# Fused attention and two MoE layers: raw weights loaded from ScalarE's queue, v loaded from SyncE's, and product runs placed behind the scores

## The chip, the cores and the metric

The kernel runs on one NeuronCore of a Trainium2 chip, as one launch. The core has a matrix engine (TensorE, PE in the profile, whose weight loads are shown as PEld), VectorE (DVE), ScalarE (ACT), GpSimd (POOL) and SyncE (SP), which run side by side and wait for each other through semaphores. A DMA is issued by an engine's sequencer: SPq is SyncE's queue, ACTq ScalarE's. The metric is the time of one execution on the device in microseconds; a kernel's number is the median of its runs.

## The reference, cut to what matters

```python
scores = 1/sqrt(64) * q @ k.T                    # q, k, v: 4 batches, 8 heads, 576 rows, 64 columns
scores = where(scores >= max(scores) - tau, scores, -1e9)
attn = exp(scores - max(scores));  attn = attn / (sum(attn) + 1e-9)
x = heads_side_by_side(attn @ v)                 # 2304 tokens x 512
h = relu(x @ w_in);  x = (s * h*h + b) @ w_out   # the first two-layer stage, width 2048
h = x @ w2_in;  out = (h * tanh(softplus(h))) @ w2_out
```

The weights arrive as 64-bit floats. q, k, v are 32-bit.

## The kernel before, in words

**Attention.** Two heads are handled together as a pair; there are 16 pairs of 9 units. A unit's scores (`scores`, 4 or 8 matmuls of 288 columns, tile S) are read by VectorE (ns, with the row maximum), ScalarE takes exp (e), VectorE masks and sums, GpSimd scales. Seven units later `weights_t` transposes a block (T), ScalarE copies it out (te), and twice in a pair `products_v` multiplies: a run of 12 matmuls after block 6, a run of 8 after block 8, both into pv. `split_x` then rounds pv into a high part xh and a rest xl. Once in a pair, at units 2 and 4, `prep_qk` transposes the next pair's k and q (tpk, tpq), splits them (hik, lok, hiq, loq) and moves them into KH, KL and Q by DMAs of SyncE; the last of these DMAs is remembered as `self.moved`.

**First weights.** 32 pieces of w_in and w_out are converted by `split_w`, a generator that `split_all` advances by one step for each new piece. In step 0 a piece is loaded into a slot of tile wraw (four slots); in step 2 ScalarE scales its high words, in step 3 VectorE puts the words together in three operations (wa), in step 4 ScalarE rounds it (wp) and VectorE takes the rest. The first MoE stage of batch 0 multiplies straight from wp; a copy is stored in DRAM for the other batches. The first steps are taken during the attention of pairs 0 to 3, the others one for each 4 parts of the first MoE stage of batch 0.

**Order.** The first four pairs run alone (while the pool `s2p` is open). After that the attention of the later pairs and the first MoE stage (`moe1`, groups of 12 matmuls h and y) are traced side by side, in the proportion of their work, and the scheduler orders each engine's instructions by its own estimate of time. Each engine and each queue then runs its list in that order; one that waits holds all behind it. `issue_after(ins)` puts an instruction behind `ins` on the same engine; `keep_in_program_order` keeps the marked instructions of an engine in the order in which they are written. Two such rules matter here: in `split_w` the load of a piece stands behind `self.moved` on SyncE, and ScalarE's scaling is kept in program order. The second MoE stage (qX, qY, qV, o) follows from 782 us on.

**v.** `load_raw` loads a pair's v by three DMAs into one of two buffers. Pairs 0 and 1 are loaded at the start from SyncE; each later pair from ScalarE's queue, written behind the products of the pair that used the buffer last.

Of the kernel before, what the change touches and what calls it, by code (L numbers as in the profile page):

```python
# [19 lines left out]
class Fused:  # L20
# [26 lines left out]
    def split_w(self, src, hi, lo, pool, tags, kw):  # L47

        nc = self.nc
        i = self.nd
        self.nd += 1
        n = src.shape[1] * src.shape[2] // 2
        raw = pool.tile([P, n, 2], I32, tag=tags[0], name=f"wraw{i}", **kw)
        with self.tc.issue_after(self.moved):
            nc.sync.dma_start(raw.rearrange("p (c f) w -> p c (f w)", c=src.shape[1]), src)  # L60
        low, high = raw[:, :, 0], raw[:, :, 1]
        hf = high.bitcast(F32)
        yield
        yield
        a = pool.tile([P, n], I32, tag=tags[1], name=f"wa{i}")
        self.tc.keep_in_program_order(nc.scalar.activation(hf, hf, AF.Copy, scale=2.0 ** -112))
        yield
        nc.vector.tensor_scalar(a, high, 3, None, op0=ALU.logical_shift_left)
        nc.vector.scalar_tensor_tensor(a, low, 29, a, op0=ALU.logical_shift_right, op1=ALU.bitwise_or)
        nc.vector.scalar_tensor_tensor(a, high, -0x80000000, a, op0=ALU.bitwise_and, op1=ALU.bitwise_or)  # L70
        yield
        af = a.bitcast(F32).rearrange("p (c f) -> p c f", c=src.shape[1])
        nc.scalar.copy(hi, af)
        (nc.gpsimd if self.s2p else nc.vector).tensor_tensor(lo, af, hi.bitcast(F32), op=ALU.subtract)
# [159 lines left out]
    def load_raw(self, pr, nm):  # L234
        nc = self.nc
        b, p = divmod(pr, self.NP)
        if b >= self.B:
            return
        src = {"q": self.q, "k": self.k, "v": self.v}[nm]
        dma = nc.scalar if nm == "q" and not pr else nc.sync  # L240
        h2 = src[b, 2 * p:2 * p + 2]

        most = h2[:, 0:512, :].rearrange("h (p c) d -> p c h d", c=4)
        if nm == "v":
            t = self.vs[pr % 2]


            dma = nc.sync if pr < 2 else nc.scalar
            dma.dma_start(t[:, :, 0:4, :], most.rearrange("p c h d -> p h c d"))
            for h in range(2):  # L250
                dma.dma_start(t[HALVES[h], h, 4, :], h2[h, 512:576, :])
        else:
            t = self.qk[nm]
            dma.dma_start(t[:, 0:4], most)
            dma.dma_start(t[0:64, 4, :, :], h2[:, 512:576, :].rearrange("h r d -> r h d"))
        self.raws[pr, nm] = t
# [69 lines left out]
    def scores(self, pr, ti):  # L326
        nc = self.nc
        Q, KH, KL, E4 = self.sets[pr % 2]
        if ti == 0:
            self.st = self.at.tile([P, 5, 9], F32, tag="stat", name=f"st{pr}", bufs=2)  # L330
        st = self.st
        nm, nthr, sm, u, rinv = (st[:, i, :] for i in range(5))
        hs = [0] if ti < 4 else [1] if ti > 4 else [0, 1]
        cols = slice(512, 640) if ti == 4 else slice((ti % 5) * 128, (ti % 5) * 128 + 128)
        S = self.s_tile(f"S{pr}_{ti}")
        for hf in range(2):
            ks = slice(hf * 288, hf * 288 + 288)
            so = S[:, hf * HB:hf * HB + 288]
            terms = [(h, K[h]) for h in hs for K in (KH, KL)]
            for i, (h, kt) in enumerate(terms):  # L340
                c0 = ti * 128 + 64 * h if ti <= 4 else 64 + ti * 128
                nc.tensor.matmul(so, Q[:, c0:c0 + 128], kt[:, ks], start=(i == 0), stop=(i == len(terms) - 1))  # L342
        ns = self.at.tile([P, 576], F32, tag="ns", name=f"ns{pr}_{ti}", bufs=2)
        sv = S.rearrange("p (h n) -> p h n", h=2)[:, :, :288]
        c1 = slice(ti, ti + 1)
        nc.vector.tensor_scalar(ns.rearrange("p (h n) -> p h n", h=2), sv, -0.125, 3.0e38,  # L346
                                op0=ALU.mult, op1=ALU.min, accum_out=nm[:, c1])
        nc.vector.tensor_scalar(nthr[:, c1], nm[:, c1], self.tau_c, None, op0=ALU.add)

        if ti < 4:  # L350
            self.es[pr, ti, "pair"] = self.at.tile([P, 1152], F32, tag="e", name=f"e{pr}_{ti}", bufs=8)
        e = E4[:, 64:640] if ti == 4 else self.es[pr, ti % 5, "pair"][:, 0 if ti < 4 else 576:][:, :576]
        nc.scalar.activation(e, ns, AF.Exp, bias=nm[:, c1], scale=-1.0)  # L353
        self.es[pr, ti] = e

        def finish():
            nc.vector.scalar_tensor_tensor(e, ns, nthr[:, c1], e, op0=ALU.is_le, op1=ALU.mult, accum_out=sm[:, c1])  # L357
            if ti not in (1, 4, 8):
                return
            g = slice({1: 0, 4: 2, 8: 5}[ti], ti + 1)  # L360
            nc.vector.tensor_scalar(rinv[:, g], sm[:, g], 1.0e-9, None, op0=ALU.add)
            nc.vector.reciprocal(rinv[:, g], rinv[:, g])  # L362

            nc.vector.tensor_scalar(u[:, g], sm[:, g], 0.5, 1.0 / self.S, op0=ALU.is_lt, op1=ALU.mult)
            for j in range(g.start, g.stop):
                t = self.es[pr, j]
                nc.gpsimd.tensor_scalar(t, t, rinv[:, j:j + 1], u[:, j:j + 1], op0=ALU.mult, op1=ALU.add)  # L367

        return finish
# [24 lines left out]
    def products_v(self, pr, chunks, tes, first, last):  # L394

        if first:
            self.pv = self.pvp.tile([P, 1024], F32, tag="pv", name=f"pv{pr}")
        v = self.vs[pr % 2]
        ins = None
        for c in chunks:  # L400
            for hf, h in ((0, 1), (0, 0), (1, 1), (1, 0)):
                te = tes[4 if c == 4 else c + 5 * h]
                args = (self.pv[HALVES[h], hf * HB:hf * HB + 288], v[:, h, c, :], te[:, hf * 288:hf * 288 + 288])
                kw = dict(start=first and c == chunks[0], stop=last and c == chunks[-1])
                if ins is None:
                    ins = self.nc.tensor.matmul(*args, **kw).ins
                else:
                    with self.tc.issue_after(ins):
                        ins = self.nc.tensor.matmul(*args, **kw).ins  # L409
        return ins  # L410
# [11 lines left out]
    def attention(self):  # L422
# [3 lines left out]
        nc = self.nc  # L426
# [14 lines left out]
        for k in range(N + LAG + 2):  # L441
            pr, ti = divmod(k, 9)
            if k < N:
                nxt = self.scores(pr, ti)
                if k < 12:
                    self.busy(warm[:, :256], 3)
                if fin:
                    fin()
                fin = nxt
                yield 550  # L450
                if pr + 1 < self.B * self.NP and ti in (2, 4):
                    self.prep_qk(pr + 1, "kq"[ti // 2 - 1])
                    yield 500
            elif fin:
                fin()
                fin = None
            j = k - LAG
            run = None
            if todo:
                tp, tc, te = todo  # L460
                tes[tc] = te
                if tc == 6:
                    run = self.products_v(tp, (1, 4, 0), tes, True, False)
                    yield 1460
                elif tc == 8:
                    run = self.products_v(tp, (3, 2), tes, False, True)
                    yield 970
                    self.split_x(tp)
                    self.load_raw(tp + 2, "v")
            todo = None  # L470
            if 0 <= j < N:
                prj, ci = divmod(j, 9)
                todo = prj, ci, self.weights_t(prj, ci, run)
                yield 550
# [461 lines left out]
```

## Time and profile before

| | |
|---|---|
| time, median of 3 runs | 1146.13 us (1144.81 to 1146.3) |
| profiled execution, its own time | 1139.95 us |
| its span, first to last instruction | 1138.2 us |
| mean granted clock of TensorE | 0.993 |
| busy: PE, DVE, ACT, POOL | 1084.1, 791.6, 620.6, 256.4 us |

A span is divided in stages by what runs: 0 to 140 us attention alone, 140 to 320 attention beside batch 0 of the first MoE stage with the conversion of its weights, 320 to 660 attention beside batches 1 and 2, 660 to 682 the last attention, 682 to 782 batch 3, and from 782 the second MoE stage. In the views, a wait is the idle time of an engine before an instruction, and behind the arrow stands what ended it. Line numbers are those of the kernel before.

### The profile page before, as it was taken

How to read it: one execution, taken by the hardware profiler on the slowest of the kernel's cores; microseconds unless marked ns; L12 is line 12 of the kernel's file. 1: busy time of each engine (PE TensorE's matmuls, PEld its weight loads, DVE VectorE, ACT ScalarE, POOL GpSimd, SP SyncE). 2: the span in 40 equal slices, each digit the busy share in tenths (PEclk: the TensorE clock that was granted, in tenths of full speed). 3: DMA queues.
4: the chain of work that ended last, by engine and by line, in shares of the span. 5: the costliest groups of instructions: out<-in, count | busy, mean ns of one | idle time of the engine just before them, and what ended most of it. 6: DMA issues, size and time to landing. Idle time of an engine off the chain costs nothing.

```text
span 1138.2 us, 21403 instructions
## 1 busy us (share of the span) xinstructions
PE 1084.1 (95%) x7964; PEld 1018.2 (89%) x7964; DVE 791.6 (70%) x1746; ACT 620.6 (55%) x1153; POOL 256.4 (23%) x306
## 2 busy tenths in 40 slices
PE   7887999998899999999999989999999999999998
PEld 7765789887798989899889879999999999999998
DVE  5988766879776676867776767654787377825782
ACT  4656686756566656557646557643454144513351
POOL 3543334252332433415243210300000000000000
PEclk9999999999999999999999999999999999999999
DMA  7376385656887678887974589985999999997783
GB/s 160 87 180 187 103 239 186 227 158 215 237 275 250 213 222 247 286 256 241 328 228 138 193 299 341 394 340 217 351 387 346 335 413 387 338 338 260 265 296 121
DMA packets 141591, 292.70 MB, mean 257 GB/s; under 512 B 52848, under 2 KB 78960, under 8 KB 133168
## 3 DMA queue, kind: packets, MB, share of 16 engines
q1 hardware_dynamic: 134256, 286.91, 74.9%
q10 hardware_dynamic: 7232, 4.43, 1.4%
q8 instruction: 63, 1.03, 0.4%
q14 instruction: 40, 0.33, 0.1%
HBM read 201.85 MB, written 66.58 MB: 236 GB/s over the span
## 4 chain that ended last, share of the span: by engine, by line
PE 59%; DVE 8%; DMA 6%; ACT 3%; issue 2%; POOL 2%; SPq 1%; DVEq 0%; ACTq 0%; POOLq 0%
PE o L747 16%; PE y L502 11%; PE h L502 9%; PE qY L613 7%; PE qX L613 4%; PE qV L613 4%; PE pv L409 2%; PE S L342 2%; DMA wsi<-chli 2%; PE T L380 2%; POOL e L367 1%; DVE e L357 1%; DMA wso<-chlo 1%; DVE ns L346 1%; DMA wraw<-in_moe_w_out_dram 1%
## 5 line engine op out<-in xcount | busy, mean ns | idle before, releaser
L367 POOL TENSOR_SCALAR e<-e,st 128x576 f32<-128x576 f32 x128 | 134.1, 1059 | 212.1 <-DVE st L362 187.4
L747 PE MATMUL o<-wo,hl 128*128 128x256 f32 x1512 | 177.9, 279 | 0.0
L747 PEld LDWEIGHTS o<-wo,hl 128*128 128x128 f32 x1512 | 177.5, 188 | 0.0
L502 PE MATMUL h<-xh,w 128*128 128x288 f32 x768 | 164.5, 299 | 4.4 <-ACT r L523 1.4
L502 PE MATMUL y<-gh,w 128*128 128x288 f32 x768 | 165.5, 300 | 0.0
L357 DVE SCALAR_TENSOR_TENSOR e<-ns,st,e 128x576 f32<-128x576 f32 x128 | 118.6, 927 | 36.0 <-ACT e L353 35.2
L346 DVE TENSOR_SCALAR_CACHE_REDUCE ns<-S 128x576 f32<-128x576 f32 x144 | 107.8, 751 | 48.8 <-PE S L342 48.3
L353 ACT ACTIVATE e<-ns,st 128x576 f32<-128x576 f32 x128 | 99.0, 776 | 65.4 <-DVE ns L346 55.3
L502 PEld LDWEIGHTS h<-xh,w 128*128 128x128 f32 x768 | 125.7, 188 | 7.1 <-ACT r L523 2.6
L502 PEld LDWEIGHTS y<-gh,w 128*128 128x128 f32 x768 | 127.1, 190 | 0.1
L526 POOL TENSOR_TENSOR gl<-rr,gh 128x288 fp32r<-128x288 f32 x96 | 85.6, 898 | 171.3 <-ACT rr L525 165.8
L391 ACT COPY te<-T 128x576 f32<-128x576 f32 x144 | 91.4, 635 | 58.8 <-PE T L385 42.1
L502 PE MATMUL y<-gl,w 128*128 128x288 f32 x384 | 114.4, 298 | 1.8 <-POOL gl L526 1.8
L502 PE MATMUL h<-xl,w 128*128 128x288 f32 x384 | 113.5, 296 | 0.0
L380 PE MATMUL T<-ident,e 128*128 128x128 f32 x576 | 96.6, 284 | 16.0 <-ACT te L391 12.6
L342 PE MATMUL S<-KH,Q 128*128 128x288 f32 x320 | 96.9, 320 | 12.2 <-DVE ns L346 4.7
L380 PEld LDWEIGHTS T<-ident,e 128*128 128x128 f32 x576 | 69.4, 144 | 35.7 <-issue 16.3
L342 PE MATMUL S<-KL,Q 128*128 128x288 f32 x320 | 90.8, 300 | 0.0
L409 PE MATMUL pv<-te,rawv 128*64 128x288 f32 x576 | 87.2, 410 | 0.0
L613 PE MATMUL qY<-yc,wi 128*128 128x384 f32 x432 | 86.6, 337 | 0.7 <-DVE g L636 0.7
L342 PEld LDWEIGHTS S<-KH,Q 128*128 128x128 f32 x320 | 62.0, 194 | 19.3 <-DVE ns L346 7.6
L613 PEld LDWEIGHTS qY<-yc,wi 128*128 128x128 f32 x432 | 75.6, 188 | 1.3 <-DVE g L636 1.3
(150 smaller groups left out, 2186.8 us busy)
## 6 DMA issues: line engine op xcount, KB each, us to landing
w<-w SPq DMA_DIRECT2D x96, 512.0 KB, 5.5
wo<-wso SPq DMA_DIRECT2D x42, 1024.0 KB, 7.4
wi<-wsi SPq DMA_DIRECT2D x23, 1024.0 KB, 7.8
wi<-wsi SPq DMA_DIRECT2D x25, 768.0 KB, 7.3
w<-wp SPq DMA_DIRECT2D x32, 512.0 KB, 5.0
wsi<-chli SPq DMA_DIRECT2D x24, 512.0 KB, 5.0
wso<-chlo SPq DMA_DIRECT2D x24, 512.0 KB, 6.2
ycd<-yp SPq DMA_DIRECT2D x14, 768.0 KB, 7.8
```

Source lines behind the costliest of these rows:

```text
L342: nc.tensor.matmul(so, Q[:, c0:c0 + 128], kt[:, ks], start=(i == 0), stop=(i == len(terms) - 1))
L346: nc.vector.tensor_scalar(ns.rearrange("p (h n) -> p h n", h=2), sv, -0.125, 3.0e38, op0=ALU.mult, op1=ALU.min, accum_out=nm[:, c1])
L353: nc.scalar.activation(e, ns, AF.Exp, bias=nm[:, c1], scale=-1.0)
L357: nc.vector.scalar_tensor_tensor(e, ns, nthr[:, c1], e, op0=ALU.is_le, op1=ALU.mult, accum_out=sm[:, c1])
L367: nc.gpsimd.tensor_scalar(t, t, rinv[:, j:j + 1], u[:, j:j + 1], op0=ALU.mult, op1=ALU.add)
L380: nc.tensor.transpose(T[:, i * 128:i * 128 + 128], self.es[pr, i, "pair"][:, o:o + 128], self.ident)
L391: nc.scalar.copy(te, T[:, :576])
L409: ins = self.nc.tensor.matmul(*args, **kw).ins
L502: nc.tensor.matmul(acc[:, :n], w[:, wl, c], rhs[c][xl][:, ts], start=(i == 0), stop=(i == 11))
L526: (nc.vector if b == 3 else nc.gpsimd).tensor_tensor(gl[:, ts], r2, gh[:, ts].bitcast(F32), op=ALU.subtract)
L613: self.nc.tensor.matmul(acc, a, b, start=(first and i == 0), stop=(i == n - 1), skip_group_check=True)
L747: nc.tensor.matmul(bank[p][t], hl[:, gl, j, ts], w[:, 2 * (q % 2) + j, wl], start=(old is None and q + j + k == 0), stop=(q + j + k == 6), ...
```

## The change

Three things are changed. The load of a raw weight piece is issued by ScalarE and kept in its program order, where it was issued by SyncE behind the last k or q move. v is loaded by SyncE for every pair, for pairs 2 to 14 behind the k moves of the next pair (at unit 2 of the pair itself), for pair 15 at its unit 2, where it was loaded by ScalarE behind the products two pairs before. And the first matmul of a product run stands behind the last scores traced so far, once the first four pairs are over.

```diff
@@ split_w
-        with self.tc.issue_after(self.moved):
-            nc.sync.dma_start(raw.rearrange("p (c f) w -> p c (f w)", c=src.shape[1]), src)
+        self.tc.keep_in_program_order(nc.scalar.dma_start(raw.rearrange("p (c f) w -> p c (f w)", c=src.shape[1]), src))
@@ load_raw
-            dma = nc.sync if pr < 2 else nc.scalar
@@ scores
-                nc.tensor.matmul(so, Q[:, c0:c0 + 128], kt[:, ks], start=(i == 0), stop=(i == len(terms) - 1))
+                self.scored = nc.tensor.matmul(so, Q[:, c0:c0 + 128], kt[:, ks], start=(i == 0), stop=(i == len(terms) - 1)).ins
@@ products_v
-                    ins = self.nc.tensor.matmul(*args, **kw).ins
+                    with self.tc.issue_after(self.scored) if not self.s2p else nullcontext():
+                        ins = self.nc.tensor.matmul(*args, **kw).ins
@@ attention
+                if pr + 1 == self.B * self.NP and ti == 2:
+                    self.load_raw(pr, "v")
                 if pr + 1 < self.B * self.NP and ti in (2, 4):
                     self.prep_qk(pr + 1, "kq"[ti // 2 - 1])
+                    if ti == 2 and pr >= 2:
+                        with self.tc.issue_after(self.moved):
+                            self.load_raw(pr, "v")
...
                     self.split_x(tp)
-                    self.load_raw(tp + 2, "v")
```

The built lists of the engines show what moves. First SyncE's queue in the kernel before, at the k and q moves of pair 7 (wraw13 to wraw16 are weight pieces, rawq is a later pair's q, w1 a stored piece):

```order
L303 DMA KL11_130<-lok7_2176 64x576
L60 DMA wraw13_2202<-in_moe_w_in_dram 128x4x256
L60 DMA wraw14_2271<-in_moe_w_out_dram 128x4x256
L254 DMA rawq_111<-in_q_dram 128x8x64
L255 DMA rawq_111<-in_q_dram 64x2x64
L303 DMA Q1_125<-hiq7_2303 64x576 x2
L303 DMA Q1_125<-loq7_2304 64x576 x2
L60 DMA wraw15_2367<-in_moe_w_out_dram 128x4x256
L60 DMA wraw16_2425<-in_moe_w_out_dram 128x4x256
L195 DMA w1_0_2_1_2508<-wp0_2_1_2192 128x1024
```

Pieces 13 and 14 stand behind the k moves, 15 and 16 behind the q moves. In the changed kernel the same loads stand on ScalarE, each behind the scaling (L65) of the piece two before it; here two steps in a row:

```order
L72 CAST wp0_2_2_2579<-wa18_2771 128x512
L65 ACTIVATE wraw20_2773<-wraw20_2773 128x512
L59 DMA wraw22_2936<-in_moe_w_out_dram 128x4x256
L525 ACTIVATE gh0_2_1_2659<-r0_2_1_0_2696 128x288
L526 ACTIVATE rr0_2_1_0_2697<-r0_2_1_0_2696 128x288
L278 CAST hiq7_2303<-tpq7_2294 128x640
L525 ACTIVATE gh0_2_1_2659<-r0_2_1_1_2734 128x288
L526 ACTIVATE rr0_2_1_1_2735<-r0_2_1_1_2734 128x288
L72 CAST wp0_2_3_2670<-wa19_2854 128x512
L65 ACTIVATE wraw21_2856<-wraw21_2856 128x512
L59 DMA wraw23_3014<-in_moe_w_out_dram 128x4x256
```

The rounding (L72) of piece 18, whose slot piece 22 takes, is ahead of that load. At the q of pair 7 ScalarE is at piece 22, where SyncE's queue before was at piece 15. On SyncE the three v loads of a pair stand behind the k moves of the next pair, ahead of the next q load (here pair 8's last k move, pair 7's v, two stores of pieces, then a q load):

```order
L299 DMA KL01_122<-lok8_2785 64x576
L245 DMA rawv1_136<-in_v_dram 128x2x256
L247 DMA rawv1_136<-in_v_dram 64x64 x2
L194 DMA w1_1_2_3_3505<-wp1_2_3_3147 128x1024
L194 DMA w1_0_3_2_3587<-wp0_3_2_3231 128x1024
L250 DMA rawq_111<-in_q_dram 128x8x64
```

Before, these three loads stood on ScalarE's queue. On TensorE, the first product run of pair 5 before, which follows the transposes of pair 7's q; the scores S6_5 come 27 rows behind its first row:

```order
L274 MATMUL tpq7_2294<-ident_72,rawq_111 128x64
L272 MATMUL tpq7_2294<-ident_72,rawq_111 128x128 x4
L274 MATMUL tpq7_2294<-ident_72,rawq_111 128x64
L406 MATMUL pv5_2369<-te5_6_2324,rawv1_136 64x288
L409 MATMUL pv5_2369<-te5_1_2007,rawv1_136 64x288
```

And in the changed kernel, where the same run follows those scores:

```order
L503 MATMUL y0_1_1_0_2839<-gh0_1_3_2494,wp1_1_1_2357 128x288
L338 MATMUL S6_5_2334<-KH01_120,Q0_117 128x288
L338 MATMUL S6_5_2334<-KL01_122,Q0_117 128x288
L338 MATMUL S6_5_2334<-KH01_120,Q0_117 128x288
L338 MATMUL S6_5_2334<-KL01_122,Q0_117 128x288
L403 MATMUL pv5_2369<-te5_6_2324,rawv1_136 64x288
```

The scores of a unit are issued about one unit earlier against products and transposes, in every pair after the fourth.

## Rows read from the trace of the kernel before

**Rows 1.** The page: busy time by engine; then the last-ending chain by engine.
```profile
PE 1084.1 (95%) x7964; PEld 1018.2 (89%) x7964; DVE 791.6 (70%) x1746; ACT 620.6 (55%) x1153; POOL 256.4 (23%) x306
PE 59%; DVE 8%; DMA 6%; ACT 3%; issue 2%; POOL 2%; SPq 1%; DVEq 0%; ACTq 0%; POOLq 0%
```

**Rows 2.** Windows: stretch, length; busy PE, PEld, DVE, ACT, POOL; clock; DMA; GB/s.
```profile
0.00:140.00 140.00, 115.28 (x782) 95.08 (x783) 110.60 (x328) 79.52 (x122) 57.94 (x85) 0.95 0.56 142
140.00:320.00 180.00, 166.86 (x1266) 151.86 (x1265) 139.49 (x346) 120.38 (x238) 62.75 (x82) 1.00 0.69 211
320.00:660.00 340.00, 332.47 (x2522) 306.85 (x2521) 242.60 (x606) 212.09 (x426) 124.53 (x131) 0.99 0.75 238
660.00:682.00 22.00, 18.12 (x134) 14.48 (x134) 11.97 (x25) 10.88 (x19) 0.00 (x0) 1.00 0.96 344
782.00:1138.20 356.20, 351.99 (x2520) 350.85 (x2518) 225.78 (x330) 138.05 (x213) 0.00 (x0) 1.00 0.87 321
```

**Rows 3.** Waits of PE from 140 to 320: total us, times, longest us.
```profile
PE tpq L274 <- DVE ns L346: 3.3, 2, 2.4
PE T L380 <- ACT te L391: 2.9, 2, 2.3
PE S L342 <- DVE ns L346: 2.0, 2, 1.2
PE y L502 <- ACT wp L73: 1.5, 1, 1.5
PE y L502 <- ACT r L523: 1.4, 1, 1.4
```

**Rows 4.** Timeline of SyncE's queue: start, length, instruction.
```profile
255.89 1.75 SPq L60 DMA_DIRECT2D wraw<-in_moe_w_out_dram  x3
```

**Rows 5.** Chain that ended last, in order of time: start, length, what.
```profile
243.81 4.79 DMA wraw<-in_moe_w_in_dram
248.62 0.68 ACT wraw L66
249.32 0.43 DVE wa L68
```

**Rows 6.** Timeline of PE, three instructions that waited: idle time and releaser in brackets.
```profile
250.47 0.43 PE L274 MATMUL tpq<-ident,rawq 128*128 128x64 f32 x2 [2.42 <-DVE ns L346]
...
264.83 0.40 PE L502 MATMUL y<-gh,wp 128*128 128x288 f32 x1 [1.45 <-ACT wp L73]
...
312.19 0.66 PE L380 MATMUL T<-ident,e 128*128 128x128 f32 x4 [2.34 <-ACT te L391]
```

**Rows 7.** Waits of ACT and DVE for the raw weights, 140 to 320.
```profile
ACT wraw L66 <- DMA wraw<-in_moe_w_out_dram: 14.0, 10, 2.9
...
DVE wa L68 <- ACT wraw L66: 16.9, 8, 3.9
```

**Rows 8.** Tiles rawv and wraw: issues (ns min/median/max, first, last), landing time.
```profile
L251 ACTq DMA_DIRECT2D rawv<-in_v_dram x28: 472/514/1303, 47.1 to 592.5; - x28
L249 ACTq DMA_DIRECT2D rawv<-in_v_dram x14: 368/372/464, 53.8 to 602.4; - x14
...
L60 SPq DMA_DIRECT2D wraw<-in_moe_w_in_dram x16: 367/504/964, 61.7 to 268.2; - x16
...
DMA to landing us min/median/max: 3.8/5.6/9.4
```

**Rows 9.** Timeline of ACT: an exp that stood behind a v load.
```profile
128.57 0.77 ACT L353 ACTIVATE e<-ns,st 128x576 f32<-128x576 f32 x1 [4.56 <-PE pv L409]
```

**Rows 10.** Timeline of SyncE's queue, moves of pair 3's q and what precedes them.
```profile
61.73 0.59 SPq L60 DMA_DIRECT2D wraw<-in_moe_w_in_dram  x1
```

**Rows 11.** Waits of PE from 320 to 660.
```profile
PE y L502 <- POOL gl L526: 1.8, 1, 1.8
...
PE T L380 <- POOL e L367: 1.0, 2, 0.6
PE T L380 <- ACT te L391: 1.0, 2, 0.7
```

## The prediction

> **What bounds the kernel now.** I read the page's busy line and chain first, then the windows by stage, then TensorE's waits inside the one stage that the change touches most, and from there the queue that caused them. TensorE is busy 95% and has 59% of the chain [rows 1], so the time can fall only where TensorE idles. The windows say where that is [rows 2]: idle is length less PE busy, 24.7 us before 140 us, 13.1 from 140 to 320, 7.5 from 320 to 660, 3.9 from 660 to 682, and 4.2 in the 356 us after 782. The change cannot reach the last stage. No engine beside TensorE is full in the middle stages: VectorE is busy 139.5 of 180 us and ScalarE 120.4 [rows 2]. So the 13.1 us are waits for something late, not for something overloaded.
>
> What is late is the weight conversion. The reader is to follow one case. SyncE issues a raw piece at 243.81, right behind the k moves; it lands 4.79 us later, ScalarE scales it at 248.62 and VectorE starts on it at 249.32 [rows 5]. VectorE's list is in order, so the read of a score tile behind it waits too, and the tile is what TensorE needs: it stands still 2.42 us and starts at 250.47 [rows 6]. The next burst is three loads at 255.89 [rows 4]; it ends in 1.45 us without wp at 264.83 [rows 6]. The third ends in 2.34 us without a free transpose tile at 312.19, since ScalarE's copy stood behind a scaling whose piece had not landed [rows 6]. In the stage ScalarE waits 14.0 us in 10 waits for w_out pieces, VectorE 16.9 us in 8 for the scaling [rows 7]. Loads take a median of 5.6 us to land [rows 8]; they are late because they are issued late, two to six at a time behind a pair's moves.
>
> **Raw loads on ScalarE.** This removes the pin behind the moves and adds 32 issues to ScalarE's list. Each load now stands right behind the scaling of the piece two before it, so it has one whole step and part of another, and a step is 180 us over some 24 pieces, 7.5 us. Against a landing of 5.6 us [rows 8] that is enough, with some 5 us over on average. The slot is free by then: its rounding is ahead in the list. Bounds for the gain: 0, if VectorE's total work of 139.5 us re-forms the same waits elsewhere, and 13.1 us, all idle of the stage [rows 2]. The three cases followed add up to 6.2 us (2.42 + 1.45 + 2.34) [rows 6], and the waits for ns of 3.3 and 2.0 and for r of 1.4 [rows 3] hold others of the same kind, made by the bursts. I take 7.0 us, between the three cases and the whole, near the cases.
>
> The issues themselves: 32 of 0.504 us [rows 8] are 16.1 us of ScalarE's sequencer. The v loads that leave it were 28 of 0.514 and 14 of 0.372 us [rows 8], 19.6 us. ScalarE gets 3.5 us lighter over the kernel, but the weight-conversion stage gets heavier: 24 of the issues, 12.1 us, against some 5 pairs of v loads of 1.4 us, 7.0 us. These 5.1 us lie beside 59.6 us in which ScalarE is idle there [rows 2]. I cost them at nothing; without that cover they are 5.1 us.
>
> The Trainium skill, page "DMA: Bandwidth & Descriptors", section "Issuing engines are not separate DMA queues", says that DMAs issued from ScalarE, SyncE and GpSimd run on the same 16 engines and interleave, and that issuing from several saves no more than sequencer time. By that sentence the change gives nothing but issue time, which is off TensorE's path, and the sum would be zero for this part. The trace agrees that the transfers are not what is scarce (the DMA engines are busy 0.69 of the stage [rows 2]), but what it shows as late is the moment of issue, 243.81, behind other entries [rows 5], which the sentence does not price. The rival of no change below has its own price from rows.
>
> **v on SyncE.** It takes from ScalarE the waits in which it stood behind a v load until products had ended. The longest of the prologue is 4.56 us before an exp [rows 9]. Bounds for one such wait: 0, since the transposed block that ScalarE copies next stands behind the same products on TensorE anyway, and 4.56. Most are of the first kind; I take 1.0 us for all. On SyncE the loads are three issues, 1.4 us by the durations on ScalarE [rows 8], behind the k moves and ahead of the next q load. With pair 3 SyncE is issuing without a pause and the weight load in that place took 0.59 us [rows 10], so q's moves there come 0.8 us later, and these are waited for. Later pairs find SyncE idle ahead of the q load. The buffer of v is free then, the products that read it being over four units before, so nothing queues behind a wait, and v is used 12 units later. Together 0.2 us gained, rounded to 0.
>
> **Products behind scores.** No instruction is added. A run of 12 or 8 matmuls moves behind 4 or 8 score matmuls, so the scores, and with them the chain from ns to e to the transposes, get about one unit of lead. What can go are waits of transposes for e and te from 320 to 660: 1.0 for POOL's e and 1.0 for te [rows 11], 2.0 us. The bounds: 7.5 us gained, all the stage's idle [rows 2], and 2.0 lost, if the score tile, of which there is one, makes VectorE's read the new wait; the waits for ns that this would copy were 2.0 us in the weight stage [rows 3]. The 1.8 us for gl [rows 11] is a MoE wait and stays. I take 2.0 us gained. The tail from 660 to 682 idles 3.9 us [rows 2]; a group or two of MoE matmuls remains as filler beside the last transposes. I take 1.0, from 0 to 3.9.
>
> **Sum.** 7.0 + 0 + 2.0 + 1.0 = 10.0 us, from 1139.95 us of the profiled execution (span 1138.2 and 1.75 us around it) to 1129.95. That execution was 6.18 us shorter than the median of the runs, 1146.13. The time to be compared is such a median, so the same 10.0 us are taken from it: **1136.1 us**.
>
> **Rivals.**
> - More goes: the bursts also made the waits for ns and r, the prologue loses part of its 24.7 us, and the tail goes whole. All of 13.1, 7.5 and 3.9 is 24.5 us, 1121.6. For it: no engine is full. Against it: VectorE is busy 110.6 of the first 140 us [rows 2], and a schedule with three new orders makes new small waits. I price it at 20 us, 1126. Chance 0.12.
> - No change: VectorE does the same 139.5 us in the weight stage, and what it no longer waits for the loads it waits for elsewhere, or the change is issue time and no more. That is 1146.1. Against it stand the followed cases, in which both ScalarE and VectorE were idle. Chance 0.11.
> - Slower: ScalarE is held by its own loads. In the built lists 24 of the 32 carry a wait for the semaphore of an earlier DMA, most of them SyncE's k, q or v loads and moves, which in turn wait for TensorE. If the earlier DMA has not landed, te, exp, r and wp stand behind the load. A ScalarE wait of that kind cost TensorE 2.34 us at 312.19 [rows 6]. From 5 such holds on, the gain is gone (5 x 2.34 = 11.7); a third of the 24, 8 holds, is 18.7 us less 10.0, 8.7 slower: 1154.8. For it: v loads on the same queue did hold ScalarE by 4.56 us [rows 9]. Against: in the lists, the awaited DMA was mostly issued some ten ScalarE instructions earlier. Chance 0.13.
>
> **How the numbers follow.** The forecast has 0.64. Its own range, from half the sum to the sum with the stage's whole 13.1, is 1130 to 1141. The range that holds 8 in 10 reaches up over the case of no change, 1148, and down to where half of the rival of more lies, 1124. A difference under 0.2%, 2.3 us, can't be told from none here. Faster: 0.64 + 0.12 = 0.76; same 0.11; slower 0.13.
>
> **What the profile after would show.** Right: raw loads on ScalarE's queue one by one, each landed before its scaling, so that ScalarE's and VectorE's waits for raw pieces fall from 14.0 and 16.9 us [rows 7] to a few; TensorE's idle in the weight stage under 7 us; transposes of the later stages without waits for POOL's e; the stage from 782 as long as before, 356 us. Wrong: idle of TensorE put down to te, r or wp with ScalarE standing before a raw load's issue; or the raw waits gone while TensorE's idle stays near 13 us with VectorE full; or new waits of score matmuls for ns after 320 us, which would say that the earlier scores only moved the wait.

## The result, and the profile after

The changed kernel takes 1131.27 us (median of 4 runs, 1130.48 to 1133.57) against 1145.47 us for the kernel before in the same series (4 runs, 1138.06 to 1146.3): ratio 0.9894, 95% interval 0.9865 to 0.9924. That is 8.7 to 15.5 us faster; the forecast was 1136.1 us, 10.0 us faster. The kernel before scatters: in the later series, 17 runs each, it took 1136.6 to 1148.1 us, with medians from 1142.93 to 1143.75. Its profiled execution, 1139.95, lies in the lower part of that scatter. The profiled execution of the changed kernel, 1133.57 us with a span of 1131.8, is the longest of its runs. The two profiles are therefore 6.4 us apart, less than the medians.

The page of the changed kernel (busy time, then the chain of work that ended last) beside [rows 1]:

```profile
PE 1081.1 (96%) x7964; PEld 1018.7 (90%) x7964; DVE 806.3 (71%) x1746; ACT 619.0 (55%) x1153; POOL 263.4 (23%) x306
PE 67%; DVE 3%; DMA 3%; ACT 2%; issue 1%; POOL 0%; DVEq 0%; ACTq 0%; POOLq 0%
```

DMA's share of the chain went from 6% to 3%, VectorE's from 8% to 3%, and SyncE's queue, 1% before, is gone from it. The windows of the changed kernel, in the stretches of [rows 2], then the whole first part and the last stage by its own bounds (columns: stretch, length; busy PE, PEld, DVE, ACT, POOL; clock; DMA share; GB/s):

```profile
0.00:140.00 140.00, 110.64 (x738) 90.35 (x738) 107.14 (x314) 75.21 (x114) 52.84 (x79) 0.91 0.60 151
140.00:320.00 180.00, 176.97 (x1361) 163.93 (x1360) 158.47 (x368) 123.94 (x246) 74.42 (x88) 1.00 0.74 226
320.00:660.00 340.00, 332.35 (x2539) 307.49 (x2539) 251.20 (x614) 216.87 (x436) 127.11 (x131) 0.99 0.73 237
660.00:682.00 22.00, 18.05 (x136) 15.94 (x133) 11.97 (x24) 13.52 (x33) 0.00 (x0) 1.00 0.95 359
0.00:772.78 772.78, 728.17 (x5444) 667.64 (x5444) 580.46 (x1416) 480.29 (x940) 263.36 (x306) 0.98 0.73 231
772.78:1131.80 359.02, 352.91 (x2520) 351.09 (x2520) 225.80 (x330) 138.75 (x213) 0.00 (x0) 1.00 0.85 319
```

And the last two of the kernel before by its own bounds:

```profile
0.00:781.70 781.70, 731.82 (x5445) 667.01 (x5445) 565.83 (x1416) 482.30 (x940) 256.40 (x306) 0.99 0.72 228
781.70:1138.20 356.50, 352.29 (x2520) 351.15 (x2520) 225.78 (x330) 138.32 (x213) 0.00 (x0) 1.00 0.87 321
```

TensorE's idle time is length less busy. From 140 to 320 it fell from 13.1 to 3.0 us. Before 140 us it rose from 24.7 to 29.4. From 320 to 660 (7.5, now 7.7) and from 660 to 682 (3.9, now 4.0) it did not move. In the whole first part the idle time fell by 5.3 us (49.9 to 44.6) and TensorE's busy time by 3.7 (731.8 to 728.2), and the last stage became 2.5 us longer: 5.3 + 3.7 - 2.5 = 6.5, the difference of the spans (6.4) but for rounding. A window with fixed bounds holds other work in another kernel, as the counts in brackets show, so the sums over the whole first part weigh more than those of one stage.

What became of the weight pieces is read best from the tile wraw, where the view says who waited for it (us, times). The kernel before, whole span, then the changed kernel:

```profile
  DVE wa L68: 21.5, 9
  ACT wraw L66: 19.7, 14
  ACT wp L73: 8.6, 10
```

```profile
  ACT wp L72: 3.3, 2
  DVE wa L67: 2.4, 1
```

ScalarE's scaling (L66 before, L65 now) no longer waits for a piece at all. ScalarE's timeline in the changed kernel shows why (start, length, engine and line; idle before in brackets):

```profile
222.23 0.37 ACTq L59 DMA_DIRECT2D wraw<-in_moe_w_out_dram  x1
...
223.23 0.69 ACT L65 ACTIVATE wraw<-wraw 128x512 f32<-128x512 f32 x1
...
226.51 0.37 ACTq L59 DMA_DIRECT2D wraw<-in_moe_w_out_dram  x1
...
233.55 0.38 ACTq L59 DMA_DIRECT2D wraw<-in_moe_w_in_dram  x1
...
234.19 0.68 ACT L65 ACTIVATE wraw<-wraw 128x512 f32<-128x512 f32 x1
```

One load stands in each step, and the piece loaded at 222.23 is scaled two steps later, at 234.19, 12 us after its issue. The piece of [rows 5] was scaled 4.8 us after its issue, when it had just landed. Of TensorE's waits from 140 to 320, where [rows 3] had 3.3, 2.9, 2.0, 1.5 and 1.4 us, these are left:

```profile
PE S L338 <- DVE lok L279: 1.0, 1, 1.0
PE tpq L270 <- DVE ns L342: 0.9, 1, 0.9
PE y L503 <- DVE y L550: 0.5, 1, 0.5
PE y L503 <- ACT r L524: 0.4, 1, 0.4
PE pv L403 <- ACT te L387: 0.2, 1, 0.2
```

### The profile page after: what moved, and what is told of

It is laid out like the page before. It is cut to its first block, busy times and chain, and to the rows that moved or that the text cites. A ratio compares the mean times of both kernels' runs of the same rounds, so it can differ in the third digit from the quotient of the medians.

```text
span 1131.8 us, 21384 instructions
## 1 busy us (share of the span) xinstructions
PE 1081.1 (96%) x7964; PEld 1018.7 (90%) x7964; DVE 806.3 (71%) x1746; ACT 619.0 (55%) x1153; POOL 263.4 (23%) x306
## 4 chain that ended last, share of the span: by engine, by line
PE 67%; DVE 3%; DMA 3%; ACT 2%; issue 1%; POOL 0%; DVEq 0%; ACTq 0%; POOLq 0%
PE o L748 16%; PE y L503 13%; PE h L503 12%; PE qY L614 6%; PE qX L614 4%; PE qV L614 4%; PE S L338 3%; PE pv L406 3%; PE T L376 3%; DMA wso<-chlo 1%; DMA wi<-wsi 1%; PE pv L403 1%; PE T L381 1%; DMA w<-w 1%; ACT e L349 0%
## 5 line engine op out<-in xcount | busy, mean ns | idle before, releaser
L353 DVE SCALAR_TENSOR_TENSOR e<-ns,st,e 128x576 f32<-128x576 f32 x128 | 114.9, 899 | 22.6 <-ACT e L349 21.6
L527 POOL TENSOR_TENSOR gl<-rr,gh 128x288 fp32r<-128x288 f32 x96 | 93.6, 989 | 128.8 <-ACT rr L526 128.8
L376 PE MATMUL T<-ident,e 128*128 128x128 f32 x576 | 92.5, 283 | 15.3 <-ACT te L387 14.7
```

Source lines behind the costliest of these rows:

```text
L376: nc.tensor.transpose(T[:, i * 128:i * 128 + 128], self.es[pr, i, "pair"][:, o:o + 128], self.ident)
L527: (nc.vector if b == 3 else nc.gpsimd).tensor_tensor(gl[:, ts], r2, gh[:, ts].bitcast(F32), op=ALU.subtract)
```

## The experiments

All times are medians; a ratio is that of the runs to the runs of the kernel before in the same series, with its 95% interval. Three theories stood against each other. A: the gain is the weight pieces that no longer land late. B: it is the scores ahead of the product runs. C: it is ScalarE without v's loads.

**raw_only**, the first part of the change alone:

```diff
-        with self.tc.issue_after(self.moved):
-            nc.sync.dma_start(raw..., src)
+        self.tc.keep_in_program_order(nc.scalar.dma_start(raw..., src))
```

> Only the raw weight loads are moved to ScalarE; v's loads and the product runs are as before. Theory A (the gain is the weight pieces that no longer land late): 7 to 12 us under the kernel before, TensorE's idle from 140 to 320 us down from 13.1 to 3 to 5 us. Rival B (the gain comes from the scores standing ahead of the product runs): within 2.3 us of before. Rival C (the gain comes from ScalarE no longer standing behind v loads): within 2.3 us, or slower, since ScalarE now holds both kinds of load.

Measured 1131.73 us, ratio 0.9905 (0.9881 to 0.9929), 8.1 to 13.6 us faster. A holds: this part alone is as fast as the whole change. Its window:

```profile
140.00:320.00 180.00, 177.12 (x1355) 163.12 (x1355) 151.72 (x354) 124.49 (x248) 75.13 (x90) 1.00 0.76 231
```

Idle from 140 to 320 is 2.9 us.

**v_only**, the second part alone:

```diff
-            dma = nc.sync if pr < 2 else nc.scalar
...
+                    if ti == 2 and pr >= 2:
+                        with self.tc.issue_after(self.moved):
+                            self.load_raw(pr, "v")
```

> Only v's loads are moved to SyncE. Theory A: within 2.3 us of before, or 1 to 3 us slower, since SyncE's queue, in which the weight pieces come late, gets three more entries per pair. Rival B: within 2.3 us. Rival C: 8 us or more faster than before.

Measured 1143.68 us, ratio 0.9997 (0.9976 to 1.0018): nothing. C falls.

**scores_only**, the third part alone:

```diff
+                    with self.tc.issue_after(self.scored) if not self.s2p else nullcontext():
+                        ins = self.nc.tensor.matmul(*args, **kw).ins
```

> Only the product runs are put behind the scores. Theory A: 0 to 3 us faster than before, since the waits for the weight pieces stay. Rival B: 8 us or more faster. Rival C: within 2.3 us.

Measured 1152.02 us, ratio 1.0074 (1.0050 to 1.0099), 5.7 to 11.3 us slower. B falls, and so does the gain that A expected here. Its windows:

```profile
0.00:140.00 140.00, 112.00 (x761) 92.70 (x762) 109.94 (x325) 77.02 (x117) 57.98 (x85) 0.93 0.56 142
140.00:320.00 180.00, 164.25 (x1197) 147.77 (x1196) 131.44 (x323) 116.23 (x231) 64.46 (x82) 0.95 0.65 200
```

The idle time from 140 to 320 is 15.8 us against 13.1, and the granted clock there is 0.95 against 1.00. The longest wait of that stage in TensorE's timeline, and the same piece on SyncE, ScalarE and VectorE:

```profile
255.32 0.43 PE L272 MATMUL tpq<-ident,rawq 128*128 128x64 f32 x2 [3.02 <-DVE ns L344]
```

```profile
248.56 0.59 SPq L60 DMA_DIRECT2D wraw<-in_moe_w_in_dram  x1
```

```profile
253.48 0.65 ACT L66 ACTIVATE wraw<-wraw 128x512 f32<-128x512 f32 x1 [3.11 <-DMA wraw<-in_moe_w_in_dram]
```

```profile
254.16 0.43 DVE L68 TENSOR_SCALAR wa<-wraw 128x512 int32<-128x512 int32 x1 [4.44 <-ACT wraw L66]
254.51 0.75 DVE L344 TENSOR_SCALAR_CACHE_REDUCE ns<-S 128x576 f32<-128x576 f32 x1
```

It is the case that the prediction followed at 243.81, with a longer wait: the piece is issued behind the k moves at 248.56, scaled at 253.48, and the score tile is read behind it.

This stage is not shown to be where the 8.5 us are lost, though. v_only, which lost nothing, has the same idle time there, 15.8 us, and nearly the same clock; first its stage, then the whole first part of scores_only:

```profile
140.00:320.00 180.00, 164.20 (x1184) 145.38 (x1183) 127.31 (x318) 112.57 (x222) 62.97 (x80) 0.96 0.64 198
0.00:792.26 792.26, 735.22 (x5444) 671.74 (x5444) 568.58 (x1416) 483.19 (x940) 262.53 (x306) 0.97 0.71 225
```

Over the whole first part TensorE idles 57.04 us in scores_only, 49.88 in the kernel before. Of the 7.2 us more, 3.3 lie before 140 us, 2.6 from 140 to 320 and 1.3 behind; 3.4 us of busy time and 1.3 of the last stage make up the rest of the 11.9 us between the two spans. In the profiles the loss is spread over the stages.

**raw_late**, the changed kernel with the pieces of the first stage loaded as before:

```diff
+        if i < 9:
+            with self.tc.issue_after(self.moved):
+                nc.sync.dma_start(raw..., src)
+        else:
             self.tc.keep_in_program_order(nc.scalar.dma_start(raw..., src))
```

> The changed kernel, but pieces 0 to 8 are loaded by SyncE behind the k and q moves as before; from piece 9 on ScalarE loads them. Theory H (in the first 133 us ScalarE stood behind its own loads, which waited for an earlier DMA, and TensorE lost the 4.07 us at 88.83 and the 2.82 us at 125.47 by it): 4 to 8 us faster than the changed kernel, some 1125 us, the first h matmul back from 133 to some 123 us. Rival (the longer prologue comes from VectorE's order and the clock): within 2.3 us of the changed kernel. Rival (the early pieces are late again and their delay runs on): 3 us or more slower than the changed kernel.

Measured 1133.78 us, ratio 0.9912 (0.9890 to 0.9934): as the changed kernel, so the gain of H is not there. Its expectation named two waits in the changed kernel, at 88.83 and at 125.47. The second is the prediction's slower rival at work. On ScalarE and on TensorE:

```profile
121.03 0.68 ACT L65 ACTIVATE wraw<-wraw 128x512 f32<-128x512 f32 x1
124.32 0.41 ACTq L59 DMA_DIRECT2D wraw<-in_moe_w_out_dram  x1
124.77 0.64 ACT L387 COPY te<-T 128x576 f32<-128x576 f32 x1 [3.07 <-DMA rawq<-in_q_dram]
```

```profile
125.47 1.11 PE L376 MATMUL T<-ident,e 128*128 128x128 f32 x4 [2.82 <-ACT te L387]
```

ScalarE stands from 121.71 before its own load, which waits for an earlier DMA of SyncE (q), and te stands behind it. The wait at 88.83 is not of that kind: ScalarE issues no piece between 78.12 and 101.39. There te stands behind a split of q, whose wait the profile puts down to a DMA of v:

```profile
87.54 0.69 ACT L278 CAST hiq<-tpq 128x640 fp32r<-128x640 f32 x1 [2.81 <-DMA rawv<-in_v_dram]
```

The first h matmul did come back to 121.5 us, but that is no saving. The windows up to that matmul and from it to 320, raw_late:

```profile
0.00:121.50 121.50, 97.45 (x663) 80.00 (x663) 97.76 (x287) 69.26 (x105) 48.02 (x76) 0.94 0.62 153
121.50:320.00 198.50, 190.08 (x1434) 171.17 (x1435) 163.21 (x395) 130.91 (x254) 75.87 (x91) 1.00 0.72 219
```

the kernel before up to its first h matmul:

```profile
0.00:122.41 122.41, 98.58 (x662) 82.39 (x663) 97.45 (x292) 70.66 (x107) 49.53 (x77) 0.94 0.63 160
```

and the changed kernel up to its own:

```profile
0.00:133.20 133.20, 104.15 (x691) 85.24 (x692) 104.23 (x303) 72.48 (x110) 52.84 (x79) 0.91 0.63 159
```

The counts in brackets say it: 691 matmuls stand ahead of the first h in the changed kernel, 662 in the kernel before, 663 in raw_late. My reading of 133 us as a stage made 11 us longer compared stretches with different work. The idle time ahead of 320 us is 24.1 + 8.4 = 32.5 us in raw_late and 29.4 + 3.0 = 32.4 in the changed kernel.

**sp_nopin**, the kernel before with the pin taken away and nothing else:

```diff
-        with self.tc.issue_after(self.moved):
-            nc.sync.dma_start(raw..., src)
+        nc.sync.dma_start(raw..., src)
```

> The kernel before with one edit: SyncE's loads of raw weight pieces are no longer pinned behind the k and q moves; they stay on SyncE's queue. In the built list they stand one by one between the stores of finished pieces. Theory A1 (what mattered is that pieces are issued one by one and early, not which engine issues them): 8 to 14 us faster than before, ScalarE's and VectorE's waits for raw pieces from 140 to 320 us gone, and the first h matmul stays at some 122 us, since no load holds ScalarE. Rival A2 (the loads must leave SyncE, because there they stand behind stores and moves that wait): within 2.3 us of before, with waits for raw pieces of 10 us and more left.

Measured 1132.85 us, ratio 0.9898 (0.9879 to 0.9917). A1 holds: the engine that issues is not what matters. SyncE's queue now has the pieces one by one between stores:

```profile
216.45 0.37 SPq L59 DMA_DIRECT2D wraw<-in_moe_w_out_dram  x1
217.54 0.34 SPq L194 DMA_DIRECT2D w<-wp  x1
220.57 0.37 SPq L59 DMA_DIRECT2D wraw<-in_moe_w_out_dram  x1
```

and its windows:

```profile
0.00:140.00 140.00, 109.08 (x751) 89.41 (x752) 107.00 (x318) 76.43 (x116) 53.02 (x81) 0.94 0.62 160
140.00:320.00 180.00, 177.20 (x1354) 163.09 (x1354) 150.57 (x354) 122.41 (x247) 74.85 (x88) 1.00 0.73 225
```

Idle is 2.8 us from 140 to 320, and 30.9 before 140, though ScalarE has no weight load to be held by. One part of the expectation failed: the first h matmul stands at 131.4 us, not 122, since here too 692 matmuls stand ahead of it. The early idle time does not need ScalarE's loads.

**no_scores**, **no_v** and **no_raw**, the changed kernel with one of the three parts undone (the diffs above, backwards):

> The changed kernel without the third part: raw loads on ScalarE and v on SyncE, product runs as before. Theory S1 (product runs behind scores cost only where weight pieces come late; with early pieces they cost and gain nothing): within 2.3 us of the changed kernel, some 1131. Rival S2 (the runs cost some 9 us always, and v's move gives them back): 1123 to 1127 us.

> The changed kernel without the second part: raw loads on ScalarE and product runs behind scores, v on ScalarE as before. Theory S1: within 2.3 us of the changed kernel, some 1131. Rival S2: 1136 to 1141 us, and waits of some 4 us behind ScalarE's v loads as the one at 512.11 us of the kernel with the third part alone.

> The changed kernel without the first part: v on SyncE and product runs behind scores, raw pieces on SyncE behind the moves. Theory S1 (the 9 us of the third part alone come from late pieces, 8.7 us in the waits at 255, 258, 306 and 309 us): 1148 to 1154 us. Rival S2 (v's move pays for the runs): within 2.3 us of the kernel before, some 1143.

Without the third part: 1129.95 us, ratio 0.9881 (0.9860 to 0.9903). Without the second: 1133.47 us, 0.9904 (0.9883 to 0.9924). Both overlap the changed kernel (0.9865 to 0.9924): with early pieces, neither v's move nor the product runs can be told from nothing, as S1 said. Without the first: 1145.33 us, 1.0021 (1.0005 to 1.0037), 2.4 us slower than before. That all gain is gone without the first part again supports A. S1 had put this kernel at 1148 to 1154, which does not hold. S2's "within 2.3 us" lies inside the interval (0.6 to 4.2 us slower), but S2's 1123 to 1127 for no_scores and 1136 to 1141 for no_v do not hold. So neither theory holds as a whole. With v on SyncE the product runs cost 2.4 us, without it 8.5. One wait that may be in the difference is in scores_only, where ScalarE's v loads stand before te until an earlier q load has landed:

```profile
509.32 2.00 ACTq L249 DMA_DIRECT2D rawv<-in_v_dram  x2
511.42 0.64 ACT L389 COPY te<-T 128x576 f32<-128x576 f32 x1 [6.01 <-DMA rawq<-in_q_dram]
```

TensorE waits 4.03 us for that te at 512.11:

```profile
512.11 0.66 PE L378 MATMUL T<-ident,e 128*128 128x128 f32 x4 [4.03 <-ACT te L389]
```

The same wait is in no_v, as S2 had expected; it is the other kernel that has product runs behind scores and v on ScalarE. On ScalarE and on TensorE:

```profile
495.99 0.64 ACT L388 COPY te<-T 128x576 f32<-128x576 f32 x1 [5.87 <-DMA rawv<-in_v_dram]
```

```profile
496.68 0.55 PE L377 MATMUL T<-ident,e 128*128 128x128 f32 x3 [3.89 <-ACT te L388]
```

In no_raw, with v on SyncE, no te from 320 us on waits for a DMA of q or v. So some 4 of the 6.1 us may be this wait. Nothing I ran takes it alone away, and no_v, which has it, is not measurably slower than the changed kernel, so the difference stays open.

**extra_step**, the kernel before with a piece scaled one step later:

```diff
         yield
         yield
+        yield
         a = pool.tile([P, n], I32, tag=tags[1], name=f"wa{i}")
...
-        for item in list(pieces) + [None] * 4:
+        for item in list(pieces) + [None] * 5:
```

> The kernel before with one edit: a piece is scaled three steps after its load instead of two, so that the whole conversion comes one step later; loads stay on SyncE, pinned behind the moves, v and the product runs as before. Theory A1 (the time lost is the wait for pieces that land late): ScalarE's waits for raw pieces from 140 to 320 us fall from 19.8 us to under 6, and the kernel is 5 to 11 us faster than before. Rival A3 (the gain needs the loads to be spread out one by one, or finished pieces to be early): within 2.3 us of before or slower, with waits of TensorE for wp in the place of those for ns and te.

Measured 1146.72 us, ratio 1.0029 (1.0009 to 1.0049), 3.3 us slower. The edit did not do what it was for. Who waited for wraw there:

```profile
  DVE wa L69: 23.0, 9
  ACT wraw L67: 23.0, 10
```

The waits stayed. The pin still holds the pieces back: SyncE issues four in one burst behind the q moves.

```profile
259.45 0.59 SPq L304 DMA_DIRECT2D Q<-loq  x1
260.26 2.12 SPq L60 DMA_DIRECT2D wraw<-in_moe_w_out_dram  x4
```

There are also only four slots for pieces: SyncE's loads waited 15.8 us in 3 waits, from 140 to 320, for VectorE to be done with an earlier piece (15.0 in 5 in the kernel before). So this run does not tell A1 from A3; it only shows that another step of distance in the program is no cure while the pin and the four slots stand.

**late_v**, **nopin_v** and **late_start** look for a better kernel. late_v is raw_late without the third part. nopin_v is the second part on top of sp_nopin. late_start is no_scores with one more edit:

```diff
-            if k >= 42 and k % 10 == 2:
+            if k >= 52 and k % 10 == 2:
```

> The changed kernel without the product runs behind scores, and with pieces 0 to 8 on SyncE behind the moves. Theory Z (VectorE's work on the early pieces is only moved: idle taken from the first stage comes back in the next): within 2.3 us of the same kernel with all pieces on ScalarE, 1130 us. Rival H: 4 us or more faster than that, 1126 us.

> v's loads on SyncE as in the change, raw pieces on SyncE without the pin, product runs as before. Theory A1 (the engine that issues the pieces does not matter): within 2.3 us of the kernel with raw pieces on ScalarE and v on SyncE, 1130 us. Rival A2 (SyncE's queue, now with all loads of the attention stage, holds pieces or q and k): 1133 us or more.

> Raw pieces on ScalarE, v on SyncE, product runs as before, and the conversion begins ten units of attention's program later, one piece less ahead of the first MoE stage. Theory D (in the first stage TensorE waits for VectorE, which spends about 4.3 us on a piece): idle ahead of the first h matmul falls by 2 to 4 us and the kernel takes 1126 to 1128 us. Rival Z: the piece is missing later, TensorE waits for wp in batch 0, and the time is 1129 to 1134 us.

late_v: 1132.06 us, 0.9897 (0.9882 to 0.9913), so Z and not H. nopin_v: 1133.04 us, 0.9912 (0.9893 to 0.9931); the median is 3.1 us above no_scores, just past what A1 allowed and just inside A2's "1133 us or more", but the intervals overlap, so this run does not decide between them. late_start: 1126.65 us, 0.9858 (0.9840 to 0.9876), the lowest median of all, inside the time that D expected. Its window before 140 us:

```profile
0.00:140.00 140.00, 113.72 (x755) 94.57 (x755) 109.32 (x319) 76.55 (x116) 52.27 (x80) 0.91 0.60 151
```

The idle time before 140 us is 26.3 us against 29.4 in the changed kernel, but no_scores, on which this edit stands, already has 27.3. Ahead of the first h matmul the idle time fell from 26.95 us (that matmul at 129.5 in no_scores) to 25.31 (at 126.4), 1.6 us where D asked for 2 to 4. D's reason is therefore not shown. Its 4.3 us for a piece run from VectorE's first operation on it to the last; VectorE is busy with one for some 2.4 us there. The kernel is 14.2 to 18.3 us faster than the kernel before. Over the changed kernel the gain is possible, but the intervals overlap (0.9865 to 0.9876), and those of no_scores and late_start more (0.9860 to 0.9876), so it is not shown.

## Why the prediction was right, and where its steps were not

The time and the side were right, and the cause too: the pin behind the k and q moves made the pieces late, and taking it away is the whole gain (sp_nopin 0.9898, raw_only 0.9905, all three parts 0.9894). What is shown is the pin. Without it the pieces come both earlier and one by one, and no run tells these two apart. The terms were less good than their sum: the raw loads gave more than their 7.0 us, and the 3.0 us for the product runs and the tail did not come. The two errors cancel in part, and that the sum came so near is in that measure luck.

- **Raw loads, 7.0 us.** Too small. Alone they give 8.1 to 13.6 us, and the stage's idle time fell by 10.3 us in raw_only, 10.1 in the changed kernel. The step that failed is "near the cases": the three waits that I followed to a late piece were not most of the harm but a sample, and the waits for ns and r went with them: 3.3, 2.0 and 1.4 us in [rows 3], 0.9 and 0.4 now. The whole of the stage, my upper bound, was the nearer end.
- **v on SyncE, 0.** Right, by v_only (0.9976 to 1.0018).
- **Products behind scores, 2.0 us.** Wrong, and alone outside my bound of 2.0 us lost: it costs 5.7 to 11.3 us. The mechanism that I bounded it by, a wait for ns, is seen at 255.32, 3.0 us long, where I took the 2.0 us of the scores' own waits for ns [rows 3]. But it is not the loss: v_only idles as long in that stage and loses nothing. One wait that I left out is that of te behind v's loads on ScalarE, which cost TensorE 4.0 us at 512.11; from 320 us on no other kernel than scores_only and no_v has a wait of T for te over 1.6 us. In the change itself, with early pieces, the part shows neither gain nor loss. The waits of transposes from 320 to 660 that it was to take are smaller in the changed kernel, 0.8 us for 2.0 (0.5 for POOL's e, 0.3 for te). But the stage idles as long as before (7.7 us), with new waits in their place: 1.7 us for ScalarE's y and 1.3 of the k transposes for ns.
- **The tail, 1.0 us.** Not there: 3.9 us idle before, 4.0 now, and 3.8 in the 22 us of the changed kernel that end as far behind its last product (650.6 to 672.6).
- **The first stage.** I gave it no term, and spoke of it only in the rival of more, as a gain. Its idle time rose by 4.6 us in the profiles, so that of the 10.1 us only 5.3 are left over the whole first part. With pieces early the order ahead of the first h matmul changes, with ScalarE's loads (29.4 us idle) or without them (30.9 in sp_nopin).
- **The last stage "as long as before, 356 us".** It took 359.0 (356.5 before, by its own bounds). It is 359.1 in sp_nopin and 356.7 in no_scores, so the early pieces alone do not make it longer. In the changed kernel it has 1.3 us of new waits for a second-stage weight:

```profile
PE qX L614 <- DMA wi<-wsi: 1.3, 2, 1.0
```

- **TensorE's busy time.** I treated it as fixed. It fell by 3.7 us over the first part, from 731.8 to 728.2, and as much in raw_only (727.7) and sp_nopin (728.2). I can't put that on one group of instructions, so its cause is open.

Of the rivals, no change was excluded by the interval. The slower one, ScalarE held by its own loads, exists at 121.71, but a kernel without any such load is no faster, so it did not decide. The sentence of the Trainium skill, page "DMA: Bandwidth & Descriptors", section "Issuing engines are not separate DMA queues", held in what it says, that issuing from several engines saves no more than sequencer time: with the pieces issued by SyncE or by ScalarE the ratio is the same, 0.9898 and 0.9905. The zero that this part would have by it did not come, because the change of queue also took a pin away.

## What to carry to other kernels

When transfers land late, ask first what the issue stands behind. Here removing one ordering rule gave as much as moving the loads to another engine, and one more step of distance between load and use gave nothing (3.3 us slower) while the rule stood. Before a stage is called longer, count its instructions: the first h matmul came 11 us later with 29 more matmuls ahead of it. And an order that costs 5.7 to 11.3 us in one kernel can cost nothing measurable in another that differs only in when its weights land, so parts of a change are to be tried together and apart.

## What was not expected of the hardware

The kernel before, with the same instructions each time, scatters over 1136.6 to 1148.1 us in 51 runs, 17 on each of three chips (1139.7 to 1148.1 on one of them, where raw_only's six runs lie within 1130.9 to 1134.9). The mean granted clock of those 51 runs goes from 0.985 to 0.994, and the longer runs tend to have the lower one (correlation -0.61). raw_only's clocks go from 0.986 to 0.994, so the clock alone does not make the scatter.

From 140 to 320 the granted clock is 0.95 in scores_only and 1.00 in the kernel before and in raw_only. From 310 to 314 us of scores_only it is 0.50, the lower level, 1.2 GHz; in the 6 us before, TensorE had been busy 1.9 us, and from 316 on it is 1.00 again, 2.4 GHz. But it is also 0.96 from 140 to 320 in v_only, which loses nothing, and 0.94 in no_raw. How much of the 8.5 us of scores_only is clock, the runs do not say.
